# Two linear-attention blocks and two gated feed-forward blocks on one core: pass heads moved into the stage ahead, gate/up units read from the weights themselves

## The chip, the cores and the metric

One core of one Trainium2 chip runs the whole kernel in one launch. The metric is the device time of that core in microseconds (us). Times of a kernel are the median of several executions; the profile is of one execution more, whose own time stands beside its span below.

## The reference

`x` has 2048 rows (tokens) of 1024 numbers in bf16. Two kinds of block alternate, A, B, A, B, each on the normalized rows and added to `x`:

```python
x = A_x
x = x + _A_ref(_layernorm(x), A_wqkv, A_wo)
x = x + _B_ref(_layernorm(x), B_w_gate, B_w_up, B_w_down)
x = x + _A_ref(_layernorm(x), A_wqkv, A_wo)
x = x + _B_ref(_layernorm(x), B_w_gate, B_w_up, B_w_down)

def _A_ref(x, wqkv, wo):            # 32 heads of 32
    q, k, v = split(x @ wqkv)
    phi = lambda t: where(t > 0, t + 1, exp(t)) + 1e-6
    pq, pk = phi(q), phi(k)
    kv = einsum("bhsd,bhse->bhde", pk, v);  z = sum over s of pk
    o = einsum("bhqd,bhde->bhqe", pq, kv) / (einsum("bhqd,bhd->bhq", pq, z) + 1e-6)
    return heads_joined(o) @ wo

def _B_ref(x, w_gate, w_up, w_down):  # 1024 -> 3584 -> 1024
    return ((x @ w_gate) * (x @ w_up)) @ w_down
```

## The kernel before, in words

**Engines and order.** Each operation is added by `P.add(engine, ...)` in the order of the Python program; each engine works through its own operations in that order, and `P.plan` puts in the semaphore waits that reads and writes of the same bytes (`rd`, `wr`) or PSUM banks (`prd`, `pwr`) ask for. So the order of the code is the order on each engine. All DMAs, row transposes by DMA (L518, L799) among them, are issued from SyncE's one queue (SP), in order: a DMA whose wait is not met holds up those behind it.

**Block A** (`layer_A`), in stages: projections of k and q, a group of eight matmuls of 512 columns per 128 tokens and half (L767), evacuated by `phi_evac` through ScalarE and VectorE (DVE); `gchunk` (L851) with `kvt`, which make the 32x32 products of k and v; `norm(i)` (L787 to L799), which divides 128 rows of q by their sums: a product on DVE (L787), small DVE operations, a product on GpSimd (L796) into one of two buffers and a DMA transpose (L799) of it. `norm` is called for 14 row tiles (`NNORM`) in the gchunk loop and for the last two in the output stage. Four q projections are held back (`held`) and come after that loop, with `wprod` (L891, evacuated by ScalarE, or by DVE at L898), then the output stage: `y_grp` (L939), eight matmuls per 128 tokens and half. There the next block's layernorm is worked too (`nxt`, a `LN`): `start` (statistics on DVE), `b1_one`, `b2_one` (writes the normalized row into one of two buffers `xn`, by ScalarE at L447 in this stage), `step_t` (transposes it, L518, which frees the buffer). `y_seed` (L933) and the copy behind `y_grp`'s second half are ScalarE's as well; the four banks of `B_YY` go round.

**Block B** (`layer_B`) works in two passes of 1024 tokens. Each pass has a gate/up stage (`gateup`) and a down stage (`down`). Both use a fast matrix product with seven products in place of eight, on blocks of the matrices. So they need sums of weight blocks: S sums (`prep_s`), T sums of the input (`t_ops`, on DVE at L662), T products of the down weights (`wd_prep`). Some products are split once more (the sets in `L2SETS`): their sums of weights are made by `sums` in the first block's second pass and written to `sp_scratch`, and read again by `sp_load` in the second block.

The gate/up stage goes over 14 pairs of units (one of `w_gate`, one of `w_up`, 256 of the 3584 columns each). For each pair the tokens in a string of `ORDERS` are called in turn: `P1A` is product 1 of the first unit (L1016), `D..` its last product, `M..` an evacuation, `11`, `16`, `17`, `21`, `31` are steps of the twice split products (L1082, two or four matmuls of 256 columns, which ScalarE at L1097, L1107, L1125 and DVE at L1100 take on), `S1`, `S5` the sums of weights, `Ra` and `Rb` load a unit to come. A `+` means the pair after. The first pair's tokens with a `+` make the head of a pass, and it runs after the down stage (L1285) or output stage ahead has ended. In the first block's first pass (`jit`) the S sums are made as the units come in, and stored by `store_s`.

**The units.** A ring of five slots holds units of 7168 bytes per partition, and five more pieces of 1024 for block 21. `ring_issue` sends the next load. The blocks of the weights lie in a scratch tensor `w_scratch`, per unit 4096 numbers of each partition: 2048 copied from `w_gate` and `w_up` by `pack()` (L404), 2048 of the S sums. `pack()` is called between the projections and in the first four gchunks of the first block A, 28 units by two DMAs each. So a load of a unit in the three later passes is

```python
dma(vh(o, 3584), wscr[u][:, 512:4096], r_slot(n), KRR[sl], rd=R(V_S + u * 32, 32) + R(V_PK + u * 64, 64))
```

896 KB in pieces of 7168 bytes.

Of the kernel before, what the change touches and what calls it, by code (L numbers as in the profile page):

```python
# [180 lines left out]
def build_kernel(nc, A_x, A_wqkv, A_wo, B_w_gate, B_w_up, B_w_down, out):  # L181
# [3 lines left out]
    NJ = NFT // 2  # L185
# [19 lines left out]
    SZ_SLOT = 7168  # L205
    off = 0

    def take(n, align=64):
# [26 lines left out]
    O_GT = O_ZACC + 4096  # L235
    RB = take(NST * D * 2)
# [5 lines left out]
    RC = take(NR * (SZ_SLOT + 1024) + 1024)  # L242
    O_SLOT = RC + NR * 1024
# [13 lines left out]
            "1": [RB + 28672 + i * 1024 for i in range(3)], "5": [RC + 4096, RC + NR * (SZ_SLOT + 1024), O_X1]}  # L257
# [11 lines left out]
    V_PK = V_SP + NJ * 64  # L269
    P = _Prog(V_PK + 2 * NJ * 64)  # L270
# [18 lines left out]
    KPK = [dkey("pk%d" % i) for i in range(2 * NJ)]  # L289
# [3 lines left out]
    KTL = [dkey("tl%d" % i) for i in range(2)]  # L293
# [6 lines left out]
    wscr = nc.dram_tensor("w_scratch", (2 * NJ, 128, 4096), F16, kind="Internal").ap()  # L300
# [5 lines left out]
    with ExitStack() as es:  # L306
# [63 lines left out]
        B_YY = [5, 6, 7, 3]  # L370
        B_GX = [0, 1]
# [82 lines left out]
        class LN:  # L454
# [59 lines left out]
            def transpose(self, n):  # L514
                d, r = self.dst(n)
                i = self.order[n]
                if self.use_dma:
                    P.add("sp", lambda e: e.dma_start_transpose(xnT[:, :, i * 128:(i + 1) * 128], d),  # L518
                          rd=r, wr=r_xT(i * 128, (i + 1) * 128), dma_sem=KTF[i] if self.to == "A0" else KTL[n % 2])
                    return  # L520
# [72 lines left out]

        def r_slot(n, lo=0, hi=SZ_SLOT):
            o = O_SLOT + (n + 1) % NR * SZ_SLOT
            return [(o + lo, o + hi)]
# [7 lines left out]

        def sp_place(ps_, p, g):
            xp = O_X + (8 * ps_ + 3) * D * 2
            o = {"12": (xp, RC), "53": (xp + 4096, O_R + 12288)}[g][p % 2]
            return o, R(V_SP + 64 * p + 32 * SPG.index(g), 32)

        pk_n = [0]  # L610
        first_b = [True]
        sp_done = set()

        def pack():
            u = pk_n[0]
            if u >= NU:
                return
            pk_n[0] += 1
            j, m = unit_jm(u)
            w16 = wscr[u].bitcast(BF16)[:, 0:2048].rearrange("p (i k c) -> p i k c", i=2, c=128)  # L620
            for i in range(2):
                c0 = j * 256 + (1 - i) * 128
                dma(w16[:, i], wgu_v[m][:, :, c0:c0 + 128], R(V_PK + u * 64 + 32 * i, 32), KPK[u])

        def sp_load(ps_, p, g):
# [3 lines left out]
            o, rv = sp_place(ps_, p, g)  # L629
            dma(vh(o, 2048), spscr[2 * p + SPG.index(g)], R(o, 4096), KSP[g, p % 2], rd=rv)  # L630
# [4 lines left out]
        def ring_issue():  # L635
# [59 lines left out]

        def x_need(tk):
# [28 lines left out]

        def prep_s(n):
            o = r_slot(n)[0][0]
            o21 = RC + (n + 1) % NR * 1024
            sv = [wt_h(o + 3072 + i * 1024) for i in range(4)]
            a11, a12, a21, a22 = wt(o + 1024), wt(o + 2048), wt(o21), wt(o)  # L730
            r11, r12, r21, r22 = R(o + 1024, 1024), R(o + 2048, 1024), R(o21, 1024), R(o, 1024)
            rs = [R(o + 3072 + i * 1024, 1024) for i in range(4)]
# [5 lines left out]
        def store_s(n):  # L738
            u = n % NPASS
            sl = (n + 1) % NR  # L740
            dma(wscr[u][:, 2048:4096], vh(r_slot(n)[0][0] + 3072, 2048), R(V_S + u * 32, 32), KSW[sl], rd=r_slot(n, 3072, 7168))
# [16 lines left out]
        def layer_A(lnp, nxt, first):  # L758
# [65 lines left out]
            for kind, i in seq:  # L824
# [12 lines left out]
                if first and i >= 3:  # L837
                    pack()
# [62 lines left out]
            for n in range(2 * KT):  # L901
                gchunk(n)
                if first and n < 4:
                    pack()
# [11 lines left out]
                if n >= 2 and na[0] < NNORM:  # L916
# [11 lines left out]
            proj_q(*held[3])()  # L928

            def y_seed(n):  # L930
                if n < NST:
                    xs, bank = x_res[:, tok[n], 512:1024], B_YY[(2 * n + 1) % 4]
                    P.add("act", lambda e: e.copy(psb(bank), xs), rd=r_x(tok[n], 512, 1024), pwr=[bank])  # L933

            def y_grp(i, dh, n):
                bank = B_YY[(2 * n + dh) % 4]
# [18 lines left out]
            for i in range(NST):  # L955
# [4 lines left out]
                elif RG["n"] < NR:  # L960
                    ring_issue()
                nxt.step_t(1)
                nxt.b1_one()
                if i >= 2 and (first or i < 14):
                    nxt.start(i - 2)
                y_grp(tok[i], 0, i)
                y_seed(i + 1)
                nxt.b2_one()
                y_grp(tok[i], 1, i)
                if not first and i == 12:  # L970
                    for k in range(5):
                        stash(3 + k)
                if not first and i == 14:
# [6 lines left out]
                x_pop(2 if i > 11 else 1)  # L980
            nxt.use_dma = False
            nxt.on_act = False

        def layer_B(lnp, nxt, first):
            is_last = nxt is None
            lnp.use_dma = True
            lnp.on_act = False
            lnp.need(7)
            if not RG["tq"]:
# [477 lines left out]
```

## Time and profile before

| what | value |
|---|---|
| three runs (us) | 1483.78, 1486.23, 1487.76 |
| median (us) | 1486.23 |
| profiled execution, own time (us) | 1487.03 |
| its span (us) | 1485.3 |
| granted TensorE clock, mean | 0.999 |
| TensorE (PE) busy | 1459.4 us, 7830 matmuls |
| VectorE (DVE) busy | 1089.3 us |
| ScalarE (ACT) busy | 572.7 us |
| SyncE's DMA queue | 69.5% of 16 engines' span |

The span is what the profile sees of the profiled execution; 1.7 us of its time lie around it. PE works through the stages like this (us from the span's start): first block A with projections to 122, gchunk and kvt to 185, held projections and `wprod` to 198, output stage to 254; first block B with gate/up to 424, down to 509, gate/up to 677, down to 760; second block A to 990 (its output stage from 933); second block B with gate/up to 1151, down to 1236, gate/up to 1397, down to the end.

### The profile page before, as it was taken

How to read it: one execution, taken by the hardware profiler on the slowest of the kernel's cores; microseconds unless marked ns; L12 is line 12 of the kernel's file. 1: busy time of each engine (PE TensorE's matmuls, PEld its weight loads, DVE VectorE, ACT ScalarE, POOL GpSimd, SP SyncE). 2: the span in 40 equal slices, each digit the busy share in tenths (PEclk: the TensorE clock that was granted, in tenths of full speed). 3: DMA queues.
4: the chain of work that ended last, by engine and by line, in shares of the span. 5: the costliest groups of instructions: out<-in, count | busy, mean ns of one | idle time of the engine just before them, and what ended most of it. 6: DMA issues, size and time to landing. Idle time of an engine off the chain costs nothing.

```text
span 1485.3 us, 20620 instructions
## 1 busy us (share of the span) xinstructions
PE 1459.4 (98%) x7830; PEld 749.3 (50%) x7830; DVE 1089.3 (73%) x1990; ACT 572.7 (39%) x1179; POOL 216.1 (15%) x239
## 2 busy tenths in 40 slices
PE   8999989999999999999999999999999999999999
PEld 3434434444444455554444444446666445666544
DVE  7976777877766599875569769879877575777753
ACT  3332246333310155550013322477776004777400
POOL 4542632000000000000024337210000000000000
PEclk9999999999999999999999999999999999999999
DMA  8799746988885789975364437677965766777642
GB/s 269 131 171 235 160 120 156 272 262 262 261 286 184 231 260 293 295 261 204 124 213 109 132 94 149 178 180 253 283 265 199 237 210 227 261 265 253 210 172 97
DMA packets 268338, 312.78 MB, mean 211 GB/s; under 512 B 161616, under 2 KB 214608, under 8 KB 268240
## 3 DMA queue, kind: packets, MB, share of 16 engines
q1 hardware_dynamic: 268240, 311.48, 69.5%
q8 instruction: 61, 1.00, 0.3%
q14 instruction: 37, 0.30, 0.1%
HBM read 233.31 MB, written 69.21 MB: 204 GB/s over the span
## 4 chain that ended last, share of the span: by engine, by line
PE 88%; DMA 5%; DVE 5%; issue 1%; ACT 1%; POOL 1%; SPq 0%; DVEq 0%; ACTq 0%; POOLq 0%
PE ps L1016 29%; PE ps L1285 23%; PE ps L1082 14%; PE ps L767 12%; PE ps L851 5%; DMA arena<-arena 4%; PE ps L939 4%; DVE arena L787 1%; DVE arena L790 1%; DVE arena L430 1%; DMA arena<-in_A_wqkv_dram 1%; DMA arena<-sp_scratch 1%; DVE arena L662 0%; POOL arena L796 0%; PE ps L891 0%
## 5 line engine op out<-in xcount | busy, mean ns | idle before, releaser
L665 DVE SCALAR_TENSOR_TENSOR arena<-ps,arena 128x512 f16<-128x512 f32 (+2 forms) x508 | 340.5, 686 | 204.0 <-PE ps L1285 150.4
L1016 PE MATMUL ps<-arena 128*128 128x512 f16 x2016 | 478.7, 379 | 1.0 <-DVE arena L662 1.0
L662 DVE TENSOR_TENSOR arena<-arena 128x512 f16<-128x512 f16 (+4 forms) x624 | 309.3, 520 | 60.3 <-ACT arena L1125 48.8
L1285 PE MATMUL ps<-arena 128*128 128x512 f16 (+1 forms) x1568 | 339.4, 379 | 0.0
L1016 PEld LDWEIGHTS ps<-arena 128*128 128x128 f16 (+1 forms) x2016 | 192.1, 98 | 188.3 <-ACT arena L1021 13.6
L1082 PE MATMUL ps<-arena 128*128 128x256 f16 x1960 | 259.4, 273 | 6.6 <-DVE ps L1100 2.4
L1285 PEld LDWEIGHTS ps<-arena 128*128 128x128 f16 x1568 | 153.4, 98 | 185.0
L1082 PEld LDWEIGHTS ps<-arena 128*128 128x128 f16 (+1 forms) x1960 | 189.1, 98 | 90.7 <-DVE ps L1100 11.1
L767 PE MATMUL ps<-arena 128*128 128x512 bf16 x1024 | 225.4, 380 | 8.0 <-DMA arena<-arena 4.6
L1021 ACT ACTIVATE arena<-ps 128x512 f16<-128x512 f32 x224 | 133.7, 597 | 114.9 <-PE ps L1016 113.0
L576 ACT ACTIVATE arena<-ps 128x512 f32<-128x512 f32 x128 | 76.3, 597 | 243.7 <-PE ps L767 221.7
L767 PEld LDWEIGHTS ps<-arena 128*128 128x128 f16 x1024 | 99.3, 98 | 129.3 <-DMA arena<-arena 8.2
L1097 ACT COPY ps<-ps 128x256 f32<-128x256 f32 x168 | 61.8, 369 | 212.5 <-PE ps L1082 210.0
L851 PE MATMUL ps<-arena 128*128 128x512 bf16 x512 | 115.4, 379 | 0.0
L433 POOL TENSOR_SCALAR arena<-arena 128x1 f32<-128x1 f32 x64 | 21.0, 327 | 629.5 <-DVE arena L432 629.5
L939 PE MATMUL ps<-arena 128*128 128x512 bf16 x512 | 111.0, 379 | 1.1 <-ACT ps L933 1.1
L1046 ACT COPY ps<-ps 128x512 f32<-128x512 f32 x112 | 64.2, 573 | 87.7 <-PE ps L1016 52.1
L430 DVE BATCH_NORM_STATS2 arena<-arena 128x6 f32<-128x512 bf16 x128 | 88.1, 688 | 10.7 <-DMA arena<-in_A_x_dram 6.2
L796 POOL TENSOR_TENSOR arena<-arena 128x1024 f16<-128x1024 f32 x32 | 78.2, 2444 | 97.9 <-DVE arena L794 81.1
L577 DVE TENSOR_SCALAR arena<-arena 128x512 f32<-128x512 f32 x128 | 65.8, 514 | 35.6 <-ACT arena L576 34.5
L579 DVE SCALAR_TENSOR_TENSOR arena<-ps,arena 128x512 bf16<-128x512 f32 x128 | 88.5, 691 | 4.4
L1100 DVE TENSOR_TENSOR ps<-ps,arena 128x256 f32<-128x256 f32 x168 | 69.3, 427 | 27.3 <-PE ps L1082 13.7
(51 smaller groups left out, 712.7 us busy)
## 6 DMA issues: line engine op xcount, KB each, us to landing
arena<-w_scratch SPq DMA_DIRECT2D x84, 896.0 KB, 5.5
arena<-t_scratch SPq DMA_DIRECT2D x32, 896.0 KB, 5.5
arena<-sp_scratch SPq DMA_DIRECT2D x56, 512.0 KB, 5.2
arena<-in_B_w_down_dram SPq DMA_DIRECT2D x24, 896.0 KB, 5.8
w_scratch<-arena SPq DMA_DIRECT2D x28, 512.0 KB, 7.5
sp_scratch<-arena SPq DMA_DIRECT2D x28, 512.0 KB, 3.7
arena<-in_A_wqkv_dram SPq DMA_DIRECT2D x12, 1024.0 KB, 9.1
arena<-w_scratch SPq DMA_DIRECT2D x28, 384.0 KB, 6.0
```

Of the source, the lines that this page charges most:

```text
L430: P.add("dve", (lambda h: lambda e: e.bn_stats(st[j][:, 6 * h:6 * h + 6], x_res[:, i, (D // 2) * h:(D // 2) * (h + 1)]))(h), rd=r_x(i, (D ...
L579: P.add("dve", lambda e: e.scalar_tensor_tensor(out=dst_ap, in0=psb(bank), scalar=0.0, in1=etmp[r], op0=ALU.max, op1=ALU.add), prd=[bank], ...
L662: P.add("dve", lambda e: e.tensor_tensor(out=out, in0=a, in1=b, op=op), rd=rd, wr=wr, prd=prd)
L665: P.add("dve", lambda e: e.scalar_tensor_tensor(out=out, in0=a, scalar=sc, in1=b, op0=ALU.mult, op1=op1), rd=rd, wr=wr, prd=prd)
L767: return [e.matmul(psb(bank), xnT[:, k, i * 128:(i + 1) * 128], w[:, k, h * 512:(h + 1) * 512], start=(k == 0), stop=(k == KT - 1)) for k ...
L796: P.add("pool", lambda e: e.tensor_tensor(out=asb[b].rearrange("p (h c) -> p h c", c=32), in0=pbuf.rearrange("p (h c) -> p h c", c=32), in ...
L851: return [e.matmul(psb(bank), xr[:, t, j * 128:(j + 1) * 128], pk[:, h, t, :], start=(t == 0), stop=(t == NST - 1)) for t in range(NST)]
L939: return [e.matmul(psb(bank), xnT[:, g, i * 128:(i + 1) * 128], wp[:, g, dh * 512:(dh + 1) * 512], start=(dh == 0 and g == 0), stop=(g == ...
L1016: P.add("pe", lambda e: [e.matmul(psb(bank), w[:, k, :], x[:, k, :], start=(start and k == 0), stop=(k == 3), skip_group_check=True) for k ...
L1021: P.add("act", lambda e: e.activation(t, psb(bank), AF.Copy, scale=SG), prd=[bank], wr=r)
L1082: P.add("pe", lambda e: [e.matmul(psb(bank)[:, 256 * half:256 * half + 256], w[:, k, :], xx[:, k, :], start=(start and k == 0), stop=(k == ...
L1285: return [e.matmul(psb(bank), hv[:, 7 * hf + k, t * 128:(t + 1) * 128], w[:, k, :], start=(start and hf == 0 and k == 0), stop=(hf == 1 an ...
```

## The change

- `pack()`, its keys and its region go. `ring_issue` reads the blocks of the weights from `w_gate` and `w_up`: in the first pass of the first block one DMA per unit, in pieces of 512 bytes; in the other passes three per unit, blocks 1 and 2 (256 KB in pieces of 256 bytes), the S sums (512 KB in pieces of 4096 bytes), block 4 (128 KB in pieces of 256 bytes), each with a key of its own. Slots grow to 8192 bytes and hold all blocks. Where the sum buffer of group "12" lay ahead of the ring, its four parts now lie in the last 1024 bytes of four slots (`O_SX`).
- In the first block the gchunk loop calls `norm` 13 times, and the 14th comes behind the held projections.
- `LN` to block B uses four row buffers for its first ten rows. In the output stage the order of its steps is changed, and in the second block's output stage the upper eight row tiles use banks 0 to 3 (`B_YE`).
- `gateup` gives back its token list in two parts: the head (`pro`), up to the first token that is not in `early`, and the rest (`run`). `pro_step` issues head tokens up to the next PE step: one in the last row of the output stage, and one behind each of the last three groups of the first down stage's last product, per half. `layer_B` is built before `layer_A` so that the head is known there. The `ORDERS` of the second block are shuffled.
- T sums are called from the output stage by a budget (`x_budget`) from its twelfth row; the S sums of the first two units are made there (`prep_s` at rows 13 and 14 of the first block); some sum loads and stashes of `x` are issued at other places.

The diff, cut to its core:

```diff
-    SZ_SLOT = 7168
+    SZ_SLOT = 8192
+    O_XN += [O_WQ, O_WQ + D * 2]
...
-    RC = take(NR * (SZ_SLOT + 1024) + 1024)
-    O_SLOT = RC + NR * 1024
+    RC = take(NR * SZ_SLOT + 1024)
+    O_SLOT = RC
+    O_SX = [RC + i * SZ_SLOT + 7168 for i in range(NR)]
...
-                return xn[n % 2], R(O_XN[n % 2], D * 2)
+                b = self.buf(n)
+                return xn[b], R(O_XN[b], D * 2)
+
+            def buf(self, n):
+                return n % 4 if self.to == "B" and n < 10 else n % 2
...
-        def pack():
-            u = pk_n[0]
-            if u >= NU:
-                return
-            pk_n[0] += 1
-            j, m = unit_jm(u)
-            w16 = wscr[u].bitcast(BF16)[:, 0:2048].rearrange("p (i k c) -> p i k c", i=2, c=128)
-            for i in range(2):
-                c0 = j * 256 + (1 - i) * 128
-                dma(w16[:, i], wgu_v[m][:, :, c0:c0 + 128], R(V_PK + u * 64 + 32 * i, 32), KPK[u])
...
             if u < NU:
+                j, m = unit_jm(u)
+                src = wgu_v[m][:, :, j * 256:(j + 1) * 256]
                 if RG["first"] and ps_ == 0:
-                    dma(vh(RC + sl * 1024, 512), wscr[u][:, 0:512], R(RC + sl * 1024, 1024), KRS[sl], rd=R(V_PK + u * 64, 64))
-                    dma(vh(o, 1536), wscr[u][:, 512:2048], r_slot(n, 0, 3072), KRR[sl], rd=R(V_PK + u * 64, 64))
+                    dma(vb(o, 2048).rearrange("p (k c) -> p k c", c=256), src, R(o, 4096), KRR[sl])
                 else:
-                    dma(vh(o, 3584), wscr[u][:, 512:4096], r_slot(n), KRR[sl], rd=R(V_S + u * 32, 32) + R(V_PK + u * 64, 64))
+                    dma(vb(o + 1024, 1024).rearrange("p (k c) -> p k c", c=128), src[:, :, 0:128], R(o + 1024, 2048), KRR[sl])
+                    dma(vh(o + 3072, 2048), wscr[u], R(o + 3072, 4096), KRT[sl], rd=R(V_S + u * 32, 32))
+                    dma(vb(o, 512).rearrange("p (k c) -> p k c", c=128), src[:, 4:8, 128:256], R(o, 1024), KRS[sl])
                 return
...
+        def x_budget(w):
+            while XQ and w > 0:
+                w -= 3 if XQ[0][0][0] == "t" else 1
+                x_pop()
...
-                if n >= 2 and na[0] < NNORM:
+                if n >= 2 and na[0] < NNORM - first:
                     norm(tok[na[0]])
                     na[0] += 1
...
             proj_q(*held[3])()
+            if na[0] < NNORM:
+                norm(tok[na[0]])
+                na[0] += 1
+
+            def y_bank(n, dh):
+                return (B_YY if n < 8 or first else B_YE)[(2 * n + dh) % 4]
...
-                elif RG["n"] < NR:
+                elif i > 11 and RG["n"] < NR:
                     ring_issue()
                 nxt.step_t(1)
-                nxt.b1_one()
-                if i >= 2 and (first or i < 14):
-                    nxt.start(i - 2)
                 y_grp(tok[i], 0, i)
+                if i < NST - 1:
+                    nxt.b1_one()
+                if i and (first or i < 12):
+                    nxt.start(i - 1)
                 y_seed(i + 1)
-                nxt.b2_one()
+                if i < NST - 1:
+                    nxt.b2_one()
+                if i == NST - 1:
+                    pro_step(pro, 1)
                 y_grp(tok[i], 1, i)
...
-                x_pop(2 if i > 11 else 1)
+                if i > 10:
+                    x_budget(5)
+                if first and i in (13, 14):
+                    prep_s(i - 13)
...
+        def pro_step(pro, n):
+            for _ in range(n):
+                k = len(P.streams["pe"])
+                while pro and len(P.streams["pe"]) == k:
+                    pro.pop(0)()
...
+                seq = [(it, tk) for it in range(-1, NP) for tk in order
+                       if tk[0] == "R" or 0 <= it + {"'": -1, "+": 1}.get(tk[-1], 0) < NP]
+                early = ("11", "16", "17", "P1", "21", "26", "27", "31", "36", "37", "S1", "S5", "T0", "T1", "Ra", "Rb")
+                npro = 0 if jit else [tk[:2] in early for _, tk in seq].index(False)
+                pro = [(lambda x=x: emit(*x)) for x in seq[:npro]]
...
+                def run():
+                    pro_step(pro, len(pro))
+                    for x in seq[npro:]:
+                        emit(*x)
+                    return tail
+                return pro, run
...
+                            if q == "3" and t:
+                                pro_step(pro, 1)
...
-            tail = gateup(0, ticks0, L2SETS[not first, 0])
...
+            pro0, run0 = gateup(0, ticks0, L2SETS[not first, 0])
+            pro1, run1 = gateup(1, ticks1, L2SETS[not first, 1])
...
+                down(0, dticks0, tail, pro1)
+                down(1, dticks1, run1())
```

More of the change, by code (lines that the diff above doesn't have):

```diff
@@ L288, in build_kernel @@
     KDR = dkey("dr")
-    KPK = [dkey("pk%d" % i) for i in range(2 * NJ)]
+    KRT = [dkey("rt%d" % i) for i in range(NR)]
     KDW = dkey("dw")
@@ L292, in build_kernel @@
     KTA = [dkey("ta%d" % i) for i in range(2)]
-    KTL = [dkey("tl%d" % i) for i in range(2)]
+    KTL = [dkey("tl%d" % i) for i in range(4)]
     KTF = [dkey("tf%d" % i) for i in range(NST)]
@@ L1158, in sums @@
                         return
-                    o, rv = sp_place(ps_, p, g)
-                    sp = vh(o, 2048).rearrange("p (i b c) -> p i b c", i=4, b=2)
+                    v, rp, rv = sp_place(ps_, p, g)
+                    sp = [v[:, i].rearrange("p (b c) -> p b c", b=2) for i in range(4)]
                     ws = []
@@ L1386, in dticks1, with run @@
                             stash(8 + k)
-            if first:
-                wd_tick(0)
-            if first:
+            pro0, run0 = gateup(0, ticks0, L2SETS[not first, 0])
+            pro1, run1 = gateup(1, ticks1, L2SETS[not first, 1])
+            def run():
+                lnp.use_dma = True
+                lnp.on_act = False
+                lnp.need(7)
+                if not RG["tq"]:
+                    XQ.extend(x_ops(0, L2SETS[not first, 0]))
+                if not is_last:
+                    nxt.use_dma = True
+                    nxt.on_act = False
                 for k in range(5):
                     stash(3 + k)
-            tail = gateup(0, ticks0, L2SETS[not first, 0])
-            if first:
-                wd_tick(2 * NJ)
-            lnp.need(NST - 1)
-            XQ.extend(x_ops(1, L2SETS[not first, 1]))
-            down(0, dticks0, tail)
-            tail = gateup(1, ticks1, L2SETS[not first, 1])
-            down(1, dticks1, tail)
-            lnp.use_dma = False
-            lnp.on_act = False
+                if first:
+                    wd_tick(0)
+                else:
+                    sp_load(0, 1, "12")
+                tail = run0()
+                if first:
+                    wd_tick(2 * NJ)
+                lnp.need(NST - 1)
+                XQ.extend(x_ops(1, L2SETS[not first, 1]))
+                down(0, dticks0, tail, pro1)
+                down(1, dticks1, run1())
+                lnp.use_dma = False
+                lnp.on_act = False
+            return pro0, run
         dh0 = D // 2
```

126 lines of the change are left out of this document (59 added, 67 removed), and 2 rows, old and new, of the table ORDERS.

## The prediction

> **What bounds the kernel now.** I read the page's first part first, then the busy time of each engine stage by stage, then TensorE's timeline where a stage is not full, and last the transfers. In the stage table the columns are busy time and instruction counts of PE, PEld, DVE, ACT and POOL, the granted clock, the share of the 16 DMA engines, and GB/s.
>
> ```profile
> span 1485.3 us, 20620 instructions
> PE 1459.4 (98%) x7830; PEld 749.3 (50%) x7830; DVE 1089.3 (73%) x1990; ACT 572.7 (39%) x1179; POOL 216.1 (15%) x239
> ```
> ```profile
> 0.00:17.00 17.00, 11.87 (x54) 4.90 (x55) 8.48 (x17) 5.05 (x7) 5.23 (x22) 1.00 0.94 304
> ...
> 60.00:122.00 62.00, 57.25 (x262) 24.85 (x260) 48.97 (x90) 19.31 (x33) 27.61 (x29) 1.00 0.98 171
> ...
> 183.00:198.00 15.00, 10.55 (x49) 4.43 (x47) 12.39 (x21) 4.58 (x8) 7.48 (x4) 0.89 0.72 165
> ...
> 508.00:516.00 8.00, 5.83 (x35) 2.93 (x34) 5.05 (x13) 3.54 (x9) 0.00 (x0) 1.00 0.98 289
> 516.00:676.00 160.00, 160.00 (x927) 90.49 (x926) 134.42 (x299) 88.44 (x188) 6.96 (x16) 1.00 0.88 272
> ...
> 933.00:990.00 57.00, 55.87 (x260) 25.23 (x259) 43.44 (x86) 32.42 (x44) 13.22 (x26) 1.00 0.74 192
> 990.00:1004.00 14.00, 11.85 (x85) 7.64 (x83) 11.19 (x26) 9.30 (x25) 0.00 (x0) 1.00 0.36 122
> ...
> 1237.00:1250.00 13.00, 11.11 (x76) 7.12 (x77) 7.75 (x18) 8.09 (x22) 0.00 (x0) 1.00 0.70 251
> ...
> 1397.00:1485.00 88.00, 85.43 (x396) 38.53 (x394) 42.56 (x56) 0.00 (x0) 0.00 (x0) 1.00 0.45 154
> ```
>
> TensorE is the bound everywhere, and the change leaves its 7830 matmuls as they are (counted in both built programs). So all that can be won is its idle time, 1485.3 − 1459.4 = 25.9 us, and what each stop costs beside that. The head of the kernel holds 5.1 us of it and the tail 2.6; neither is touched. Some 18 us are left, in seven places, all of them where one stage passes to the next, or where the first projections wait. In between PE is full (160.00 of 160.00 in 516:676), so a shorter transfer or a lighter DVE wins nothing there.
>
> The stops themselves, from PE's timeline (start, length, group, and in brackets the idle time before it and what ended it) and its waits:
>
> ```profile
> PE ps L767 <- DMA arena<-arena: 4.6, 6, 1.8
> ```
> ```profile
> 77.14 7.08 PE L767 MATMUL ps<-arena 128*128 128x512 bf16 x32 [1.75 <-DMA arena<-arena]
> ...
> 190.69 1.89 PE L891 MATMUL ps<-arena 128*128 128x512 bf16 x4 [3.53 <-DVE arena L868]
> 192.37 2.45 PE L767 MATMUL ps<-arena 128*128 128x512 bf16 x8
> ...
> 196.38 0.39 PE L891 MATMUL ps<-arena 128*128 128x512 bf16 x1 [0.92 <-DVE arena L898]
> ...
> 198.34 55.42 PE L939 MATMUL ps<-arena 128*128 128x512 bf16 x256
> ...
> 255.61 167.66 PE L1016 MATMUL ps<-arena 128*128 128x512 f16 x776 [1.00 <-DVE arena L662]
> ...
> 509.86 0.39 PE L1082 MATMUL ps<-arena 128*128 128x256 f16 x2 [0.90 <-DVE arena L662]
> 510.99 0.39 PE L1082 MATMUL ps<-arena 128*128 128x256 f16 x2 [0.74 <-ACT arena L1107]
> 511.91 1.26 PE L1082 MATMUL ps<-arena 128*128 128x256 f16 x10 [0.53 <-DVE ps L1100]
> ```
> ```profile
> 991.24 0.39 PE L1082 MATMUL ps<-arena 128*128 128x256 f16 x2 [0.81 <-ACT arena L1107]
> 992.78 1.92 PE L1082 MATMUL ps<-arena 128*128 128x256 f16 x14 [1.15 <-DVE ps L1100]
> ```
> ```profile
> 1237.47 0.39 PE L1082 MATMUL ps<-arena 128*128 128x256 f16 x2 [0.74 <-ACT arena L1107]
> 1238.54 1.92 PE L1082 MATMUL ps<-arena 128*128 128x256 f16 x14 [0.69 <-DVE ps L1100]
> ...
> 1245.24 0.83 PE L1082 MATMUL ps<-arena 128*128 128x256 f16 x6 [0.54 <-DMA arena<-sp_scratch]
> ```
>
> In a full stretch matmuls follow each other by (55.42 − 7.08) / (256 − 32) = 0.216 us, while the last of a group is shown with 7.08 − 31 × 0.216 = 0.38. So each stop costs 0.16 us more than its idle time.
>
> **The change, part by part.**
>
> *Packed copies dropped.* Today 56 copies from weights to scratch go through SP's queue between the transposes that feed the first projections. The DMA engines are full with them, and SP hangs on each transpose:
>
> ```profile
> 78.06 3.23 SPq L518 DMA_TRANSPOSE arena<-arena  x1
> 81.33 2.31 SPq L404 DMA_DIRECT2D w_scratch<-in_B_w_gate_dram  x2
> 83.68 2.81 SPq L404 DMA_DIRECT2D w_scratch<-in_B_w_up_dram  x2
> 86.53 3.70 SPq L518 DMA_TRANSPOSE arena<-arena  x1
> ```
>
> From one transpose to the next it is 86.53 − 78.06 = 8.5 us, of which the four copies take 2.31 + 2.81 and more waits in the queue; PE uses one per 7.1 us. Without the copies SP needs at most 3.7 us per transpose. What is late next is DVE, which feeds the transposes; it is busy 48.97 of 62 us, so it keeps up. Gain 4.6 + 6 × 0.16 = 5.6 us.
>
> *The moved norm.* Before the matmuls at 190.69 DVE works off a chain of norms, and the wait of 3.53 us is for it (the mask L868 stands behind the last one). Its pace and what held it up:
>
> ```profile
> 180.11 1.16 DVE L787 TENSOR_TENSOR arena<-arena 128x1024 f32<-128x1024 bf16 x1
> ...
> 183.41 1.16 DVE L787 TENSOR_TENSOR arena<-arena 128x1024 f32<-128x1024 bf16 x1
> ```
> ```profile
> POOL arena L796 <- DMA arena<-arena: 11.4, 2, 6.7
> ```
>
> One norm per 3.3 us. The 14th goes behind the held projections, so L868 comes 3.3 us sooner; and POOL's two waits of 11.4 us for transposes that share the queue with copies shrink as well, which alone would do. So the stop goes fully, with the slow matmuls behind it: four took 1.89 us where 0.38 + 3 × 0.216 = 1.03 is usual, eight 2.45 instead of 1.89, at a granted clock of 0.89. 3.53 + 0.92 + 2 × 0.16 + 0.86 + 0.56 = 6.2; I take 6.0, for the eight small products still share four banks. The norm now delays the first evacuations of the output stage by 3.3 us on DVE; a bank is needed again after three groups of eight, 3 × 1.73 = 5.2 us, so PE does not see it; if that cover fails it costs up to 1.5.
>
> *Output stage to first gate/up pass (255.6).* The weight sums of the first two units and the T sums are issued inside the output stage, where DVE has more room than behind it. What comes last then is ScalarE's evacuation and the last transpose, which no row separates. The most that can go is 1.00 + 0.16; I take 0.5.
>
> *Heads in the preceding stage.* In the first block's down stage, six PE steps of the second pass's first pair (11, 16, P1A and 17, with the sums S1 and S5 on DVE among them) now stand between the groups of the last product, each with 7 × 0.216 = 1.5 us of PE work between it and its successor; a DVE or ACT step there is 0.9 at most (the three waits). So 0.90 + 0.74 + 0.53 + 3 × 0.16 = 2.6 go. In the second block's down stage the steps 11, 16, 17, P1A, 31 and 21, and a sum load sent earlier, take the stops at 1237 to 1245: 0.74 + 0.69 + 0.54, 0.15 in a small one not shown, + 4 × 0.16 = 2.7 rounded down. At 990 only one step, 11, moves ahead of the last group of the output stage. Its ACT wait (0.81 + 0.16) goes. The join on DVE still stands behind five queued operations (five remain in the program's order), as it stands behind seven today:
>
> ```profile
> 988.90 3.47 DVE L662 TENSOR_TENSOR arena<-arena 128x512 f16<-128x512 f16 x7
> ```
>
> I keep about 0.9 of the 1.15 there and of the small rest, and take 1.3 of 2.15 + 0.5.
>
> *Four row buffers, other banks.* In 933:990 PE stands 57.00 − 55.87 = 1.13 us. There ScalarE, which also evacuates PE's banks, waits before it writes a normalized row:
>
> ```profile
> ACT arena L447 <- DMA arena<-arena: 8.9, 4, 4.2
> ```
>
> A transpose has to free one of two buffers first. With four it has two rows more time, 2 × 16 × 0.216 = 6.9 us, over the longest wait of 4.2. Gain 1.1 with the stop's own cost, rounded up to 1.3.
>
> *Units from the weights.* Each gate/up unit of the three later passes was one load of 896 KB in pieces of 7 KB. Now it is three: 256 + 128 KB in pieces of 256 bytes, and 512 KB in pieces of 4 KB. No PE time stands against it to be won (the passes are full), so it can only cost. Two stretches give bounds, the one of the copies (68 to 115 us) and the second pass (540 to 600):
>
> ```profile
> DMA packets 31751, 8.02 MB, mean 171 GB/s; under 512 B 31748, under 2 KB 31748, under 8 KB 31748
> ...
> q1 hardware_dynamic: 31748, 7.98, 101.0%
> ```
> ```profile
> DMA packets 7887, 17.24 MB, mean 287 GB/s; under 512 B 4625, under 2 KB 4625, under 8 KB 7882
> ...
> q1 hardware_dynamic: 7882, 17.18, 99.2%
> ```
>
> At 171 GB/s the 384 KB take 2.3 us, at 287 the 512 KB take 1.8; together 4.1 where 896 KB at 287 take 3.2. That is 0.9 per unit, 1.9 per pair of units, 26 us of transfer over the 14 pairs of the pass. Upper bound: all of it shows, +26 us, in the second pass only; lower bound: none. I take none: the 171 were read and written in HBM on both sides with transposes between; the pass has 12% (19 us) of its transfer time free; and the parts are issued earlier than the whole was, since the first waits only for the two products that read it. The program's order leaves 11.7 us of PE work from the release of that part to its next reader, against 7.6 for the whole before. Each unit also puts two issues more on SP's queue; behind them stand the sum loads of the later passes:
>
> ```profile
> arena<-sp_scratch SPq DMA_DIRECT2D x23, 512.0 KB, 5.7
> ```
>
> Of these, the one for the group "53" has 9.7 us of PE work from its release to its reader in the last pass. At 5.7 to land it can stand two issues ahead of it at 2.81 (the two copies above), with about 1 us left.
>
> The Trainium skill speaks against this part: "DMA: Bandwidth & Descriptors", Specifications, puts the smallest transfer at full rate at 512 bytes, with a read-modify-write below. The 171 against 287 GB/s agree in direction; by that rule the sum would lean to the +26.
>
> **Sum.** 5.6 + 6.0 + 0.5 + 2.6 + 2.7 + 1.3 + 1.3 = 20.0 us off the profiled execution's 1487.0 us (span 1485.3 and 1.7 around it), so 1467.0. The median of the three runs, 1486.2, lies 0.8 below that execution, so I forecast 1466.2.
>
> **Rivals.**
> (a) Heads still wait. If DVE and ScalarE are late in the down stages too, the steps put there stop PE inside it. Then the 2.6, 2.7 and 1.3 don't come: 1472.8. For it: DVE has 5.05 of 8 us at 508 to do in any case. Against: 1.5 us of cover for each step.
> (b) The transposes are late because of DVE, not the copies. Then 5.6 and some of the 6.0 stay: near 1474. Against: SP's rows, where a transpose is issued behind four copies.
> (c) Slower: the second pass becomes bound by transfers. Each pair has 0.12 × 12 = 1.4 us of DMA time free and is asked for up to 1.9 more; from 1.4 on it decides. With the whole 26 us the time is 1492. For it: 99.2% share at 540 to 600. Against: the same stretch's share holds packets that only wait. In between it costs some 5 to 12 us: 1471 to 1478.
> (d) The heads don't move, since tokens that aren't early stop the list. The built program shows them moved (six steps, six, and one), so this has no chance of its own.
>
> **How the numbers follow.** Forecast 0.59. Its own range is 1462 to 1470: below, the seven places hold 18.2 us of idle time, with 22 stops × 0.16 and 1.4 of slow matmuls 23 at most, and one more for the spread of runs; above, half of the 6.6 us of the three head terms is missing. (a) 0.13, (b) 0.05, (c) 0.23: 0.08 in its mild form, 0.07 that eats the gain, 0.08 beyond. About 0.3%, 4.5 us, is what a measurement of this kernel can tell from no change. Faster is 0.59 + 0.13 + 0.05 + 0.08 = 0.85; same 0.07, slower 0.08. The range runs from 1462 to 1478, over the forecast, (a), (b) and the mild (c); it leaves out the other two of (c), 0.15, and a little below.
>
> **What would show it.** Right: no PE wait on transposes in 60:122; PE idle for under 0.5 us in all between the last norm and the output stage; no stops around the two changes from down to gate/up; about 0.9 left at the second block's start; PE still full in the second pass with a DMA share over 0.95. Wrong: PE waits on weights or sum loads inside the gate/up passes, or DVE waits for unit loads in its weight sums, repeated pair by pair.

## The result, and the profile after

| kernel | runs (us) | median |
|---|---|---|
| before | 1483.78, 1484.80, 1486.23, 1487.76 | 1485.51 |
| changed | 1464.57, 1465.13, 1465.21, 1465.38 | 1465.17 |

The ratio is 0.9862, 95% interval 0.9844 to 0.9879: 20.3 us less, where 1466.2 us was forecast. The profiled execution of the changed kernel took 1464.57 us, 22.5 less than that of before. From the first part of its page:

```profile
span 1462.8 us, 20720 instructions
PE 1453.9 (99%) x7830; PEld 751.8 (51%) x7830; DVE 1090.1 (75%) x1990; ACT 572.0 (39%) x1178; POOL 225.8 (15%) x239
```

TensorE has the same 7830 matmuls and stands idle for 1462.8 − 1453.9 = 8.9 us instead of 25.9. All its waits, by line of the changed kernel, what they waited for, us in total, times, longest:

```profile
PE ps L413 <- POOL arena L409: 1.4, 1, 1.4
PE ps L780 <- ACT arena L540: 1.1, 1, 1.1
PE ps L780 <- DMA arena<-in_A_wqkv_dram: 1.1, 1, 1.1
PE ps L780 <- ACT arena L532: 0.9, 1, 0.9
PE ps L530 <- DVE arena L452: 0.7, 1, 0.7
PE ps L1104 <- DVE ps L1122: 0.5, 1, 0.5
PE ps L1104 <- ACT arena L1147: 0.2, 1, 0.2
```

The first five are the head of the kernel, the last two the start of the second block B's first pass. The wait of the projections for transposes is gone, and those for DVE's masks. The stage table (columns as in the prediction's):

```profile
60.00:122.00 62.00, 62.00 (x289) 28.09 (x287) 50.57 (x91) 21.27 (x36) 28.38 (x29) 1.00 0.37 98
...
183.00:198.00 15.00, 15.00 (x70) 6.68 (x69) 14.26 (x24) 6.07 (x11) 4.55 (x4) 1.00 0.28 62
```
```profile
502.00:662.00 160.00, 160.00 (x924) 90.22 (x923) 134.21 (x297) 87.06 (x185) 6.28 (x15) 1.00 0.97 275
933.00:968.00 35.00, 35.00 (x164) 15.84 (x162) 28.69 (x58) 22.28 (x30) 10.60 (x19) 1.00 0.69 163
968.00:982.00 14.00, 13.26 (x86) 8.08 (x85) 9.26 (x21) 8.61 (x23) 0.00 (x0) 1.00 0.88 247
1215.00:1228.00 13.00, 13.00 (x88) 8.10 (x86) 7.01 (x14) 7.77 (x21) 0.00 (x0) 1.00 0.85 262
```

TensorE is full in all of them but 968:982, where 0.74 us are left. In the second pass (502:662) the transfers' share rose from 0.88 to 0.97 with no stop. Where the starts of stages stand, first before, then after:

```profile
14.44 3.63 PE L767 MATMUL ps<-arena 128*128 128x512 bf16 x16 [1.15 <-ACT arena L534]
...
122.36 7.07 PE L851 MATMUL ps<-arena 128*128 128x512 bf16 x32
```
```profile
14.28 3.63 PE L780 MATMUL ps<-arena 128*128 128x512 bf16 x16 [1.15 <-ACT arena L540]
...
116.23 7.07 PE L862 MATMUL ps<-arena 128*128 128x512 bf16 x32
...
186.18 55.42 PE L954 MATMUL ps<-arena 128*128 128x512 bf16 x256
241.43 168.51 PE L1037 MATMUL ps<-arena 128*128 128x512 f16 x780
```

The projections went from 122.36 − 14.44 = 107.92 us to 101.95, so 5.97 less; from there to the output stage 198.34 − 122.36 = 75.98 became 69.95, 6.03 less. With the time above the usual distance of matmuls, summed at each place, the two traces compare so:

| place | forecast | the two traces |
|---|---|---|
| projections (transposes) | 5.6 | 6.0 |
| held projections (norms) | 6.0 | 6.0 |
| first block, output stage to gate/up | 0.5 | 1.2 |
| first block, second pass's head | 2.6 | 2.9 |
| second block, output stage (row buffers) | 1.3 | 1.3 |
| second block, first pass's head | 1.3 | 1.6 |
| second block, second pass's head | 2.7 | 3.0 |
| units from the weights | 0 | 0 |
| sum | 20.0 | 22.0 |

The other 0.5 of the 22.5 us are small steps, among them 0.16 ahead of the projections.

### The profile page after: what moved, and what is told of

It reads as the page before. It is cut to its first block, busy times and chain, and to the rows that moved or that the text cites. A ratio compares the mean times of both kernels' runs of the same rounds, so it can differ in the third digit from the quotient of the medians.

```text
span 1462.8 us, 20720 instructions
## 1 busy us (share of the span) xinstructions
PE 1453.9 (99%) x7830; PEld 751.8 (51%) x7830; DVE 1090.1 (75%) x1990; ACT 572.0 (39%) x1178; POOL 225.8 (15%) x239
## 4 chain that ended last, share of the span: by engine, by line
PE 99%; DMA 1%; DVE 0%; ACT 0%; SPq 0%; issue 0%
PE ps L1037 30%; PE ps L1312 23%; PE ps L780 15%; PE ps L1104 15%; PE ps L862 8%; PE ps L954 7%; DMA arena<-in_A_wqkv_dram 1%; PE ps L902 0%; PE ps L874 0%; SPq L406 0%; PE ps L538 0%; DVE arena L668 0%; ACT arena L540 0%; PE ps L886 0%; DVE arena L671 0%; DVE arena L960 0%
## 5 line engine op out<-in xcount | busy, mean ns | idle before, releaser
L435 POOL TENSOR_SCALAR arena<-arena 128x1 f32<-128x1 f32 x64 | 27.2, 425 | 643.0 <-DVE arena L434 643.0
L792 POOL TENSOR_TENSOR arena<-arena 128x512 f32<-128x512 f32 x60 | 74.7, 1249 | 87.1 <-DVE arena L585 85.7
```

## The experiments

Four kernels shared a chip each time, with the kernel before beside them: it took 1482.7 us (e1 to e4), 1482.0 (e5 to e8) and 1484.8 (e9 to e12), 2 to 5 us under the profiled execution of before. The changed kernel was not run again on these chips; its own four runs lie within 0.8 us. So a difference to it is one between chips, and where it is 1 to 2 us it counts only with the stops in the trace beside it.

### e1, e2, e3: the copies and the norm, put back

```diff
+        pkscr = nc.dram_tensor("pk_scratch", (2 * NJ, 128, 2048), BF16, kind="Internal").ap()
+        w16 = pkscr[u].rearrange("p (i k c) -> p i k c", i=2, c=128)   # pack(), called where it was; e1, e2
-                if n >= 2 and na[0] < NNORM - first:
+                if n >= 2 and na[0] < NNORM:                             # e2, e3
```

> The changed kernel with the 56 copies of the weights put back at their old places in SP's queue, into a scratch tensor that nothing reads (so only the queue and the transfers are as before; the moved norm stays moved). Theory 1, the copies held the transposes: the seven stops of the projections return, 6.0 us; at the held projections little returns, 0.2 to 1.0 us, since the chain of norms is one norm (3.3 us) shorter than the 3.5 us wait before. Time 1465.2 + 6.2 to 7.0 = 1471.4 to 1472.2. Rival (b), the transposes were late because of DVE: no stop returns, 1465.

> The changed kernel with both put back: the copies as in e1, and the 14th norm inside the gchunk loop. Theory 1: both losses return, 6.0 in the projections and 6.0 at the held projections: 1477.2. Rival: the second stop went for another reason (the other order on DVE around it): then only the 6.0 of the projections, 1471.2.

> The changed kernel with only the 14th norm put back into the gchunk loop, no copies. Theory 1 says that the copies alone were the cause, through GpSimd's waits for transposes: in the changed kernel DVE waits 4.2 us for TensorE before the last mask, and one norm takes 3.3 us, so nothing returns: 1465.2 within 0.5. Rival: the moved norm carries the gain at the held projections: 1468.5 (one norm of 3.3 us) to 1471.2 (all of it).

Measured: e1 1464.63 us (1464.34 to 1465.08), e2 1464.48 (1464.33 to 1464.81), e3 1464.89 (1464.77 to 1465.04). None is slower than the changed kernel. e3 came out as theory 1 said, but e1 and e2 went against both theories: with 56 copies in their old places between the transposes, the projections do not stop: none of TensorE's waits in either trace is for a transpose by DMA. Neither their places in SP's queue nor the work of the transfers was the cause by itself. What differed is seen in the transfers of 60 to 115 us, before and then in e1 (the last number of an issue's line is the median time from issue to landing):

```profile
w_scratch<-in_B_w_up_dram SPq DMA_DIRECT2D x15, 256.0 KB, 6.1
w_scratch<-in_B_w_gate_dram SPq DMA_DIRECT2D x14, 256.0 KB, 5.4
arena<-arena SPq DMA_TRANSPOSE x7, 6.0
```
```profile
DMA packets 42405, 11.48 MB, mean 209 GB/s; under 512 B 41405, under 2 KB 42400, under 8 KB 42400
...
pk_scratch<-in_B_w_gate_dram SPq DMA_DIRECT2D x16, 256.0 KB, 4.0
pk_scratch<-in_B_w_up_dram SPq DMA_DIRECT2D x15, 256.0 KB, 4.8
...
arena<-arena SPq DMA_TRANSPOSE x7, 4.3
```

The same copies land after 4.0 and 4.8 us where before they took 5.4 and 6.1, and the transposes between them after 4.3 instead of 6.0. The 209 GB/s hold some loads in larger pieces at the end of the window; from 68 to 100 us, where copies and transposes are alone, it is 171 GB/s before and 202 in e1. In e1 each unit's rows are 4096 bytes apart, and its two copies fill them; in the kernel before the rows are 8192 bytes apart, since the S sums have the other half.

### e5, e6, e7: the distance of the rows

```diff
-    pkscr = nc.dram_tensor("pk_scratch", (2 * NJ, 128, 2048), BF16, kind="Internal").ap()
+    pkscr = nc.dram_tensor("pk_scratch", (2 * NJ, 128, 4096), BF16, kind="Internal").ap()   # e5 (as e1), e6 (as e2); half of a row used
```
```diff
-    wscr = nc.dram_tensor("w_scratch", (2 * NJ, 128, 4096), F16, kind="Internal").ap()
+    wscr = nc.dram_tensor("w_scratch", (2 * NJ, 128, 4224), F16, kind="Internal").ap()      # e7: the kernel before
```

> As e1 (the 56 copies back in their old places, the norm moved), but the scratch rows that they write are 8192 bytes apart as in the kernel before, where e1 had 4096 apart and the copies cost nothing. Theory 2, the copies are slow because of where they write: copies at about 171 GB/s again, with packets that stall, and the stops of the projections return, 6.0 us, with 0.2 to 1.0 at the held projections: 1464.6 + 6.2 to 7.0 = 1471 to 1472. Rival: what made the copies of the kernel before slow was not the row distance (the other scratch tensor, its place, the number of semaphores): 1465, as e1.

> As e2 (copies back, 14th norm back in the loop), with rows 8192 bytes apart. Theory 2: both losses return, 6.0 + 6.0: 1476.5; against e5 this shows what the moved norm does under slow copies. Rival, as in e5: 1465.

> The kernel before with one line changed: the rows of the weight scratch are 8448 bytes apart instead of 8192 (256 bytes of padding each), nothing else. Theory 2 in its wide form (rows at a multiple of 8192 bytes collide in memory): the copies run as in e1, the stops in the projections and most of the stop at the held projections go, 10 to 12 us off the time of the kernel before. Narrow form (the copies are quick only where the two of a unit fill whole rows of 4096 bytes): no change. Rival of theory 2: no change.

Measured: e5 1467.08 us (1465.70 to 1468.84), e6 1470.66 (1469.65 to 1471.34), e7 1475.61 (1475.07 to 1476.30), which is 0.9958 (0.9944 to 0.9973) of the kernel before, 6.4 us less. The transfers of 60 to 115 us, e5 and then e7:

```profile
DMA packets 39325, 9.93 MB, mean 181 GB/s; under 512 B 39321, under 2 KB 39321, under 8 KB 39321
```
```profile
DMA packets 42532, 11.64 MB, mean 212 GB/s; under 512 B 41368, under 2 KB 42527, under 8 KB 42527
```

And e7 by stage:

```profile
60.00:122.00 62.00, 62.00 (x289) 28.11 (x288) 50.40 (x91) 21.22 (x35) 28.20 (x29) 1.00 0.97 228
...
177.00:198.00 21.00, 21.00 (x104) 9.57 (x102) 14.69 (x26) 9.80 (x17) 4.81 (x5) 1.00 0.47 134
```

So 256 bytes of padding per row make the copies of the kernel before as quick as those of e1 (from 68 to 100 us 203 GB/s in e7, 183 and 179 in e5 and e6), and both stops go with all 56 copies in place and no norm moved. The transposes land after 3.8 us in e7 and 5.6 in e5 (60 to 115 us), and GpSimd's waits for transposes, 11.4 us before, are 0.6 in e7 and 10.8 in e5 (100 to 200 us). The wide form of theory 2 stands for these two distances: rows 8192 bytes apart are slow, rows 8448 apart and full rows of 4096 are not. The slow rows show as packets that stall: of the 256-byte packets started in 60 to 115 us, one in a hundred took over 91 ns before and 84 in e6, 29 in e1 and 33 in e7, at a median of 18 in each. The Trainium skill, "DMA: Bandwidth & Descriptors", Latency and other measured facts, tells of such a loss for row pitches of 2 MiB and more (512 KiB still ran at 207 GB/s, near the full 214), where at 4 MiB a padding of 4 KiB helped and 192 bytes didn't. The runs here differ in size: a pitch of 8 KiB is enough to hurt in pieces of 256 bytes, and 256 bytes of padding to cure it. Why rows at this distance are slow was not tried; that they collide in memory is only argued.

e5 and e6 lost less than forecast, since their stops are smaller than those of the profiled execution before. Both ways give about the same size: e6, with both put back, is 5.5 us over the changed kernel, and e7 6.4 under the kernel before. TensorE's waits in e6:

```profile
PE ps L919 <- DVE arena L926: 1.5, 1, 1.5
...
PE ps L795 <- DMA arena<-arena: 1.2, 1, 1.2
...
PE ps L919 <- DVE arena L896: 1.0, 1, 1.0
```

One stop for a transpose of 1.2 us, not six with 4.6 in all; two at the held projections. The norm moved or not makes 1470.66 − 1467.08 = 3.6 us here, about the 3.3 of one norm, and nothing without slow copies (e3, e2). So the moved norm is worth something only where the transposes are slow.

### e4: no heads ahead

```diff
-                npro = 0 if jit else [tk[:2] in early for _, tk in seq].index(False)
+                npro = 0
```

> The changed kernel with no head token issued ahead: the heads of the three later passes come after the last product of the stage before, as they did; orders, sum loads and the budget of T sums stay as changed. Theory: the stops at the three places return, 2.9 (first block, second pass) + 1.6 (second block, first pass) + 3.0 (second block, second pass) less the 0.7 of the sum load, which is still sent early: 6.8, so 1472.0. Rival: the stops went because of the earlier T sums, sum loads and the other order, and the heads only use the room: under 2 us returns, 1465 to 1467.

Measured 1470.64 us (1470.41 to 1472.18), 5.5 more than the changed kernel. TensorE's timeline:

```profile
496.81 0.39 PE L1104 MATMUL ps<-arena 128*128 128x256 f16 x2 [0.90 <-DVE arena L668]
497.94 0.39 PE L1104 MATMUL ps<-arena 128*128 128x256 f16 x2 [0.74 <-ACT arena L1129]
498.86 1.27 PE L1104 MATMUL ps<-arena 128*128 128x256 f16 x10 [0.53 <-DVE ps L1122]
```
```profile
1222.14 0.39 PE L1104 MATMUL ps<-arena 128*128 128x256 f16 x2 [0.74 <-ACT arena L1129]
1223.06 1.92 PE L1104 MATMUL ps<-arena 128*128 128x256 f16 x14 [0.53 <-DVE ps L1122]
```

The stops of before are back to the digit at the first place (2.9 us with what each costs beside); 1.0 return at the second place and 2.1 at the third. The sum of 5.9 agrees with the time. At the third place the stop for the sum load (0.54, 0.7 with its cost) stays away, since that load is still sent early. The 0.6 that stay away at the second place must be due to the other order, the T sums or the sum loads; they were not tried apart. (Of the token orders only that of the second block's first pass was changed.)

### e9 and e10: row buffers, sums in the output stage

```diff
-                return n % 4 if self.to == "B" and n < 10 else n % 2
+                return n % 2                                             # e9
```
```diff
-                if i > 10:
-                    x_budget(5)
-                if first and i in (13, 14):
-                    prep_s(i - 13)
+                x_pop(2 if i > 11 else 1)                                # e10; prep_s(0), prep_s(1) after the stage
```

> The changed kernel with two row buffers again where it has four (the order of steps in the output stage and the other banks stay). Theory of the prediction: the stop in the second block's output stage returns, 1.3 us, 1465.0 + 1.3 = 1466.3. Rival: the stop went because of the other order or banks, and the buffers are not what ended it: 1465.0, no stop there.

> The changed kernel with the T sums called as before (one per row, two from the 13th) and the S sums of the first two units made after the output stage instead of in its rows 13 and 14. Theory: the stop ahead of the first gate/up pass returns, 1.2 us, and up to 0.5 at the second block's start: 1466.2 to 1466.7. Rival: the stop went because of the other order of the layernorm steps: 1465.0.

Measured: e9 1467.30 us (1467.28 to 1467.32), 2.1 over the changed kernel; e10 1469.65 (1468.21 to 1470.76), 4.5 over. e9 stops in the output stages of both blocks, the first of which had none before; its timeline there, and ScalarE's wait:

```profile
217.36 26.07 PE L954 MATMUL ps<-arena 128*128 128x512 bf16 x117 [1.05 <-ACT ps L948]
```
```profile
ACT arena L449 <- DMA arena<-arena: 3.6, 1, 3.6
```

In the second block the stop is 0.76; with 0.16 for each of the two that makes 2.1, the whole difference. The mechanism is the one forecast: ScalarE waits for a transpose, and the bank's seed behind it is late. The old order with four buffers was not run, so how much of the gain in the second block is due to the order or the banks is open. In e10 the expected place (ahead of the first block's gate/up) shows no stop; the second block's start does. TensorE's row, DVE's row beside it and the stage's row of the table:

```profile
978.45 3.60 PE L1101 MATMUL ps<-arena 128*128 128x256 f16 x16 [2.63 <-DVE arena L668]
```
```profile
975.71 4.15 DVE L668 TENSOR_TENSOR arena<-arena 128x512 f16<-128x512 f16 x9
```

```profile
968.00:980.00 12.00, 8.79 (x48) 4.86 (x48) 8.37 (x17) 3.81 (x10) 0.00 (x0) 0.89 0.98 274
```

Nine T operations are left over there, and the next head step waits until DVE has done about six of them. The idle time there, 2.63 + 0.53 us, is 2.5 more than in the changed kernel; the rest of the 4.5 are slower matmuls. Behind the stop sixteen matmuls of 256 columns took 3.60 us, where fourteen take 1.92 in the changed kernel: the granted clock was 0.89 in 968 to 980 us and 0.50 in 978 to 984. My theory for e10 named the wrong place; the rival was right that no stop comes back ahead of the first block's gate/up, but its time, 1465.0, was not.

### e8: where the small pieces begin to cost

```diff
-                    dma(vb(o + 1024, 1024).rearrange("p (k c) -> p k c", c=128), src[:, :, 0:128], R(o + 1024, 2048), KRR[sl])
+                    for a in range(2):   # 64 columns each; block 4 likewise
+                        dma(vb(o + 1024, 1024).rearrange("p (k a c) -> p k a c", a=2, c=64)[:, :, a], src[:, :, 64 * a:64 * a + 64],
+                            _seg(o + 1024, 8, 256, 128 * a, 128 * a + 128), KRX[a - 1][sl] if a else KRR[sl])
```

> The changed kernel with each small-piece load of the units (256 KB and 128 KB in pieces of 256 bytes) split into two DMAs of half the columns, so in pieces of 128 bytes: twice the packets for the same bytes, and two more issues per unit. If a packet of 128 bytes takes as long as one of 256 (18 ns), a unit takes 1536 x 18 / 16 = 1.7 us of transfer more, 48 us per pass. Theory (the second pass of the first block is near its limit of transfers, share 0.97): it becomes bound, about +40 us there, and up to 30 and 20 in the second block's passes: 1505 to 1560. Rival (the share counts packets that only wait, so much more room is left): under 5 us, 1465 to 1470.

Measured 1493.32 us (1491.16 and 1495.48): 28 us over the changed kernel, and 1.0078 (1.0055 to 1.0101) of before. By stage:

```profile
502.00:662.00 160.00, 152.08 (x868) 82.81 (x866) 128.38 (x286) 83.67 (x179) 5.95 (x14) 1.00 1.04 264
1004.00:1150.00 146.00, 139.07 (x972) 93.70 (x970) 113.67 (x226) 100.00 (x253) 4.15 (x8) 1.00 0.97 245
1260.00:1400.00 140.00, 134.83 (x930) 91.32 (x929) 99.09 (x196) 96.91 (x245) 0.00 (x0) 0.98 0.91 241
```

TensorE's largest wait, and DVE's in 500 to 676:

```profile
PE ps L1109 <- DMA arena<-sp_scratch: 13.1, 13, 2.9
```
```profile
DVE arena L673 <- DMA arena<-in_B_w_up_dram: 15.7, 7, 2.7
```

All three passes lose. In the second pass DVE's weight sums wait for units, in the others TensorE for sum loads. Those land 4.9 us after their issue (1004 to 1150 us), no later than the 5.7 of the changed kernel (982 to 1128): they are issued late, behind the unit loads in SP's queue. In SP's timeline the issues of unit loads take 111 of these 146 us, in the changed kernel 40. The size lies between theory and rival: +40 for one pass was too much, under 5 too little. The theory's packet price was too high: a packet of 128 bytes took 13 ns at the median (540 to 600 us), not 18. With that an estimate from the medians is (3072 × 13 − 1536 × 18) / 16 = 0.8 us of transfer more per unit, 21 us per pass instead of 48. The two issues more per unit were not separated from the smaller pieces, so whether the transfers or SP's queue set the loss is open.

### e11 and e12: tries to be quicker

```diff
+                if i == NST - 1 and not first:
+                    pro_step(pro, 1)               # ahead of the last row's first group
-                if i == NST - 1:
+                if i == NST - 1 or i == NST - 2 and not first:
                     pro_step(pro, 1)
```
```diff
-        xload(1)
         load_w("k", 1)
+        xload(1)                                   # e12, on top of e11
```

> The changed kernel with three head steps of the second block's first pass ahead in the output stage instead of one: 11 in the last row but one, 16 and 17 in the last. Theory: the join that still came late there has a group of 1.7 us in front of it, so of the 1.24 us still lost at that place about 1.0 goes: 1464.0. Rival: the steps come too early for the sums they read (a sum load of the second block lands 5 us before its first reader, DVE's T products less) and stop TensorE inside the output stage: 1465 to 1467.

> As e11, with the second half of the first weights loaded ahead of the second row tile of x at the start, where TensorE waits 1.1 us for these weights. Theory: the half lands some 0.7 us sooner and the wait shrinks by as much: 0.7 less than e11. Rival: the row tile is then late by as much, and its transpose's wait (1.15 us) takes the gain: as e11.

Measured: e11 1464.12 us (1463.85 to 1465.31), e12 1466.38 (1465.49 to 1467.07). The waits of TensorE at the second block's start in e11, and at the head of the kernel in e12:

```profile
PE ps L1106 <- ACT arena L1149: 0.4, 1, 0.4
```
```profile
PE ps L538 <- DVE arena L452: 1.4, 1, 1.4
```

e11 stops once there, where the join's wait is gone: 0.6 us lost in its trace instead of 1.24. Its range overlaps the changed kernel's, on another chip, so a gain of time is not shown. e12 is 2.3 us slower than e11 on the same chip: the wait for the weights (0.9 in e11) goes, but the row of x that now comes later makes the transpose wait 1.4 us, and the wait ahead of the first transposes (`L530`) is 1.2 instead of 0.5. That last wait lies between 0.3 and 1.1 in the runs with an unchanged head, so this part need not be the swap's doing.

## Why the prediction was right, point by point

**The bound.** Right: TensorE's work stayed as it was, and what went is its idle time, at the seven places that the trace of before named.

**Packed copies dropped (5.6) and the moved norm (6.0).** The two traces show the sizes, but the steps behind them were in part wrong. It was not that four copies stand between two transposes: e1 has them there and loses nothing. The copies were slow because their rows lay 8192 bytes apart, and slow copies held the transposes (e7). The sizes are also those of one execution: on another chip the whole of it is worth 6.4 us (e7), not 12. (What is left between e7 and the changed kernel, 10.4 us, agrees with the 10.0 of the other five places.) The norm step said that quicker transposes alone would do, and e7 and e3 bear that out; the moved norm is worth 3.6 us only under slow copies. Rival (b), DVE late with the transposes, falls with e7, where DVE's work is as before (50.40 us busy in 60:122, 48.97 before) and the stops are gone.

**Output stage to gate/up (0.5).** Undersized, and for the wrong reason: 1.2 went, but not because of the earlier sums (e10 has no stop there). What ends it, the other order of the layernorm steps or another, was not tried apart. The earlier T sums are worth 4.5 us in the second block by e10, where the prediction gave them nothing: without them the heads there wait for DVE, and the matmuls behind that stop run at a lower granted clock, which 0.16 us per stop doesn't cover.

**Heads (6.6).** Right: no step stops TensorE inside the down stages, so rival (a) is out, and about 0.9 us was to stay at the second block's start, where 0.74 are seen. By e4 the heads themselves make 5.5 us.

**Row buffers (1.3).** Right place and mechanism. In the new order two buffers would cost 2.1 (e9), more than half of it in the first block, which had no such stop before.

**Units from the weights (0).** Right as a sum, with less room than the bound had it. The share in the second pass rose by 0.97 − 0.88 = 0.09 of 160 us, 14 us, which is 0.5 per unit where 0.9 was the estimate and 19 us were free. The 171 GB/s in that estimate was the price of the slow rows; with the 202 of e1 the same working gives 1.9 + 1.8 − 3.2 = 0.5 to 0.6. Rival (c) is real: its signs, DVE waiting for units and TensorE for sum loads, come with pieces of half the size, and cost 28 us. The Trainium skill's rule of 512 bytes ("DMA: Bandwidth & Descriptors", Specifications) leaned to +26 us here. The measurement decides: pieces of 256 bytes cost transfer time that other work hides; with pieces of 128, and two issues more, it is no longer hidden.

**The sum.** 20.0 against 22.0 at the places and 22.5 between the profiled executions. The medians differ by 20.3 because the profiled execution of before was a long one of its kernel (1487.0, median 1485.5) and that of the changed one a short one (1464.6, median 1465.2). That the forecast gain of 20.0 agrees so well with 20.3 is in part luck: the places gave 2 us more than forecast, and the two profiled executions lie 2.1 us further apart than the medians.

## What to carry to other kernels

Where one engine has all the work, sum up its idle time by place in the timeline and follow each stop to what ended last; a change that moves small dependent steps in front of the work that hides them is worth those stops and little more. A wait behind transfers says that they were late, not why: put the same transfers back with one property changed (here the distance of their rows) before the queue or the amount is blamed. A free resource wants a test by doubling: the same load in pieces half as long, with twice the packets, showed how near its limit the pass already was.

## What the runs showed of the hardware that I had not expected

Copies in pieces of 256 bytes into DRAM rows 8192 bytes apart ran at 171 to 183 GB/s (before, e5, e6; 68 to 100 us), into rows 8448 bytes apart, or full rows of 4096, at 202 to 203 (e7, e1). Kernels with the slow rows also spread more: over 4.0 us in four runs of the kernel before and 3.1 in e5, against 1.2 in e7, 0.7 in e1 and 0.8 in the changed kernel. That the rows are the reason is not shown; e10 has no copies and spreads over 2.6.

After some stops of TensorE the granted clock fell: 0.89 in 183 to 198 us before, 0.81 in 496 to 505 us of e7, 0.50 in 978 to 984 us of e10. It didn't after all of them: in 177 to 198 us of e6 TensorE stands idle for 3.0 us and the clock is 1.00.
